# Attention and two feed-forwards on one core: a leaky ramp for the weights' first pass, one-step low parts, a gate from the hyperbolic tangent, and a new order

## The chip, the cores and the metric

The kernel runs on one core of a Trainium2 chip. The metric is the time of one execution on the device in microseconds (us), lower being better. Engines are named as the profile names them: PE (TensorE), DVE (VectorE), ACT (ScalarE), POOL (GpSimd) and SP (SyncE, which here issues nearly all transfers).

## The reference

Attention with RMS-normed q and k, then a feed-forward with a SiLU gate (width 2048), then a second one with a SiLU gate times a value branch (width 1536):

```python
def _attn_ref(q, k, v, g_q, g_k):                 # (4 batches, 12 heads, 448 rows, 64)
    q_n, k_n = (rmsnorm(q, g_q), rmsnorm(k, g_k))
    scores = scale * np.matmul(q_n, k_n.transpose(0, 1, 3, 2))
    attn = np.exp(scores - np.max(scores, axis=-1, keepdims=True))
    return np.matmul(attn / (np.sum(attn, axis=-1, keepdims=True) + 1e-09), v)

def _moe_ref(x, w_in, w_out):                     # x is 1792 x 768, d_ff 2048
    h = x @ w_in
    return h * (1.0 / (1.0 + np.exp(-h))) @ w_out

def _moe2_ref(x, w_gate, w_val, w_out):           # d_ff 1536
    g = x @ w_gate
    return g * (1.0 / (1.0 + np.exp(-g))) * (x @ w_val) @ w_out
```

The five weight matrices arrive as 64-bit floats, the rest as 32-bit ones.

## The kernel before

Every large product is made from float16 parts: each operand is a high part plus a low part, and three products of parts stand for one. So the other engines have two jobs beside softmax and gates: to make parts of every operand, and to turn the 64-bit weights into 32-bit ones.

**Stages.** Attention of batch 0 runs first (its products are in float32), then the hidden half of the first feed-forward for batch 0 (`ffn1_h(0)`, 288 matmuls), which needs all of `w_in` in parts, then its output half (`ffn1_o(0)`), which needs all of `w_out`. From there on, the attention of batch b+1 runs between the matmuls of `ffn1_o(b)` and `ffn1_h(b+1)`. After the last batch comes the second feed-forward, in blocks of 512, 512, 384 and 384 tokens: block 0 by `ffn2_gv`, the others by `ffn2_seven`, which makes four products out of seven with the help of precomputed sums of weights (`make_sums`, which writes `s2d`, and `make_parts`, which writes `t2d`; both are made while blocks 0 and 1 run). `ffn2_out` closes each block.

**The weights' first pass** (`bring`, lines 998 to 1034) takes a staged block of 64-bit words as pairs of 32-bit ones. A multiply of the upper word by 2^-112 (lines 1013 to 1015, on ACT, DVE or POOL) leaves the fraction in place for a shift by three bits. The sign is lost in that shift and is carried beside it: in form "D" by two DVE instructions (a mask, line 1019, and a shift of a half word, line 1020), otherwise by one DVE shift (line 1023) and two instructions of 768 on ACT or POOL (lines 1029 and 1030). Line 1032 puts shift and rest together, line 1034 sums squares for the scale. `bring` handles 1536 words a partition at a time for `w_in` and `w_out` (8 each) and 768 for the 36 blocks of the second feed-forward.

**Low parts of weights** (`convert`, `split`): on DVE (line 979), on POOL, or, in form "E", as PE pieces of 384 columns (lines 795 and 796, a float32 product and one by the constant tile `NI`), each emptied by ACT (line 798).

**Gate of the first feed-forward** (`ffn1_h`): ACT reads a finished PSUM bank with Silu (line 1161), scales into a high part (1166), and DVE makes the low part (1174). Exponentials of softmax (line 860) and Silu live in different ACT tables, so a change between the two costs an `ACT_TABLE_LOAD`. Three PSUM banks serve `ffn1_h` and `ffn1_o` in turn.

**Low parts in the second feed-forward** take three instructions: high part on ACT (1417, 1586), difference on DVE (1418, 1587), scaling by 2^11 on ACT or POOL (1420, 1589).

**Order.** `Plan.emit` lists every engine's instructions in advance, from assumed durations, from due times and from the tables of numbers in `TUNE`; tables such as `WOL` also say which engine may take an operation (A, D, P for ACT, DVE, POOL; E for PE). Each engine then runs its list in that order. Where the list would leave PE idle for longer, the planner puts in filler products (line 1811: `NI` by itself, 512 columns, no result used).

Of the kernel before, what the change touches and what calls it, by code (L numbers as in the profile page):

```python
# [1846 lines left out]
```

## Time and profile before

| | us |
|---|---|
| median of three runs | 1187.19 |
| lowest, highest | 1184.96, 1190.58 |
| the profiled execution's own time | 1184.59 |
| its span, first to last instruction | 1182.8 |
| PE busy in the span | 1140.7 (96%) |
| DVE, ACT, POOL busy | 917.6, 749.7, 260.6 |

A busy PE is not all useful work here: fillers, and PE pieces that make low parts, count as busy. The mean granted clock is 0.996 of full speed. The stages can be told by PE's lines: float32 attention to 112 us, `ffn1_h(0)` from 112 to 185, PE pieces for `w_out` from 169 to 211, `ffn1_o(0)` from 211, the first matmul of `ffn2_gv` at 657, of `ffn2_seven` at 847.

### The profile page before, as it was taken

The page shows a single profiled execution, that of the slowest core. Times are in us where ns is not written, and L with a number is a line of the kernel's source. Part 1 is how long each engine was busy: PE and PEld are TensorE (multiplying, and loading weights), DVE is VectorE, ACT ScalarE, POOL GpSimd, SP SyncE. Part 2 cuts the span into 40 slices and gives each one's busy share as a digit, 9 for nine tenths or more (in the row PEclk, how much of TensorE's full clock was granted, in tenths as well). Part 3 has the DMA queues.
Part 4 walks back from the last instruction along what each step waited for, and adds up shares of the span by engine and source line. Part 5 has one row for each costly group of instructions (what it writes and reads, how often), then busy time and mean ns, then how long its engine had stood idle before and what let it go on. Part 6 is the DMA issues. An engine that isn't in the chain of part 4 may idle for free.

```text
span 1182.8 us, 20080 instructions
## 1 busy us (share of the span) xinstructions
PE 1140.7 (96%) x7400; PEld 675.8 (57%) x7400; DVE 917.6 (78%) x1762; ACT 749.7 (63%) x1288; POOL 260.6 (22%) x231
## 2 busy tenths in 40 slices
PE   8999998999999999999999999999999899999998
PEld 4444544454444445454555554445688668987995
DVE  5989988988588876885379978877999866774773
ACT  4888978887599856995468667574356531441440
POOL 4585222245344524531031021000000000000000
PEclk9999999999999999999999999999999899999999
DMA  9555755689979997776756878646787675463432
GB/s 212 160 132 146 242 202 154 111 193 189 201 158 180 184 203 163 149 139 136 260 176 200 295 250 298 217 157 199 237 255 249 231 247 168 161 190 117 168 130 67
DMA packets 271315, 222.59 MB, mean 188 GB/s; under 512 B 187120, under 2 KB 246000, under 8 KB 271216
## 3 DMA queue, kind: packets, MB, share of 16 engines
q1 hardware_dynamic: 271056, 221.10, 68.0%
q8 instruction: 58, 0.95, 0.3%
q14 instruction: 41, 0.34, 0.1%
q10 hardware_dynamic: 160, 0.20, 0.0%
HBM read 140.44 MB, written 38.14 MB: 151 GB/s over the span
## 4 chain that ended last, share of the span: by engine, by line
PE 34%; DMA 9%; DVE 7%; ACT 5%; issue 2%; SPq 1%; POOL 1%; ACTq 0%; DVEq 0%; POOLq 0%
PE ps L1529 12%; PE ps L1643 9%; PE ps L1155 5%; PE ps L1195 4%; DMA ATT<-y2d 3%; PE ps L1407 2%; DMA ATT<-in_moe_w_out_dram 2%; DMA t2d<-ATT 1%; DMA ATT<-s2d 1%; DMA ATT<-in_moe_w_val_dram 1%; DVE ATT L979 1%; PE ps L951 1%; ACT ATT L1034 1%; DMA ATT<-x2d 1%; PE ps L841 1%
## 5 line engine op out<-in xcount | busy, mean ns | idle before, releaser
L1155 PE MATMUL ps<-XT,W 128*128 128x448 f16 x1152 | 232.5, 352 | 2.5 <-ACT FD L1161 2.3
L1195 PE MATMUL ps<-G,W 128*128 128x448 f16 x1152 | 233.4, 352 | 1.5 <-ACT FD L1199 1.1
L1155 PEld LDWEIGHTS <-W 128*128 128x128 f16 x1152 | 112.0, 98 | 108.1 <-issue 7.9
L1195 PEld LDWEIGHTS <-W 128*128 128x128 f16 x1152 | 111.9, 98 | 108.1 <-issue 6.0
L1529 PEld LDWEIGHTS <-ATT 128*128 128x128 f16 x1458 | 130.8, 99 | 16.4 <-issue 6.5
L1529 PE MATMUL ps<-XT,ATT 128*128 128x192 f16 (+1 forms) x972 | 122.0, 257 | 6.8 <-ACT G L1549 5.7
L860 ACT ACTIVATE ER<-ps,ST 128x448 f32<-128x448 f32 x144 | 102.0, 712 | 12.2 <-DVE ATT L884 5.0
L1643 PEld LDWEIGHTS <-G 128*128 128x128 f16 x720 | 70.3, 98 | 46.9 <-issue 0.3
L1643 PE MATMUL ps<-W,G 128*128 128x384 f16 x528 | 95.8, 326 | 0.1
L851 DVE TENSOR_REDUCE ST<-ps 128x2 f32<-128x896 f32 (+1 forms) x96 | 91.7, 965 | 5.3 <-PE ps L820 2.5
L884 DVE SCALAR_TENSOR_TENSOR ATT<-ER,ST,ATT 128x448 f16<-128x448 f32 x114 | 81.1, 729 | 3.5 <-ACT ATT L876 2.8
L1407 PE MATMUL ps<-XT,W 128*128 128x512 f16 x360 | 81.6, 379 | 1.3 <-ACT FD L1199 0.6
L1529 PEld LDWEIGHTS <-W 128*128 128x128 f16 x810 | 73.0, 98 | 8.3 <-issue 3.1
L1529 PE MATMUL ps<-XT,W 128*128 128x192 f16 (+1 forms) x540 | 73.2, 256 | 2.7 <-DVE ATT L1656 1.8
L1529 PE MATMUL ps<-ER,ATT 128*128 128x192 f16 (+1 forms) x486 | 66.5, 257 | 0.0
L1407 PEld LDWEIGHTS <-W 128*128 128x128 f16 x360 | 35.2, 98 | 43.1 <-issue 3.0
L841 PE MATMUL ps<-ATT 128*128 128x448 f16 x216 | 55.3, 353 | 3.7 <-ACT ER L860 2.9
L694 POOL TENSOR_TENSOR ST<-ST 128x14 f32<-128x14 f32 x20 | 55.9, 2797 | 1.4
L1174 DVE SCALAR_TENSOR_TENSOR G<-FD,ST,G 128x448 f16<-128x448 f32 x64 | 46.7, 743 | 7.0 <-POOL G L1168 4.6
L1546 DVE TENSOR_TENSOR FD<-ps,FD 128x192 f32<-128x192 f32 (+3 forms) x90 | 41.3, 464 | 11.2 <-PE ps L1529 9.2
L1656 DVE SCALAR_TENSOR_TENSOR ATT<-ps,ST,ATT 128x384 f32<-128x384 f32 x46 | 27.6, 614 | 23.9 <-ACT ATT L1652 23.3
L951 PE MATMUL ps<-ATT 128*64 128x448 f16 x396 | 42.2, 355 | 4.0 <-DMA ATT<-ATT 4.0
(283 smaller groups left out, 2123.8 us busy)
## 6 DMA issues: line engine op xcount, KB each, us to landing
ATT<-s2d SPq DMA_DIRECT2D x36, 768.0 KB, 4.3
ATT<-in_moe_w_out_dram SPq DMA_DIRECT2D x24, 768.0 KB, 6.6
ATT<-t2d SPq DMA_DIRECT2D x36, 384.0 KB, 3.6
W<-in_moe_w_in_dram SPq DMA_DIRECT2D x16, 768.0 KB, 6.5
ATT<-in_moe_w_gate_dram SPq DMA_DIRECT2D x12, 768.0 KB, 5.7
ATT<-in_moe_w_val_dram SPq DMA_DIRECT2D x12, 768.0 KB, 5.5
y2d<-ATT SPq DMA_DIRECT2D x24, 384.0 KB, 2.9
ATT<-y2d SPq DMA_DIRECT2D x12, 768.0 KB, 5.8
```

Of the source, the lines that this page charges most:

```text
L694: op(POOL, 2600, lambda: nc.gpsimd.tensor_tensor(st["r"], st["r"], half, ALU.pow), shared=False, r=["half"], w=[("r", i)], due=due)
L841: nc.tensor.matmul(out=sp[:, u, 0:S], lhsT=T[:, 0, t, :], rhs=T[:, a, :, 64 * h:64 * h + 64], start=(a == 1), stop=(a == 2))
L851: op(DVE, 1.04 * S * nt + 65, lambda sp=sp, top=top, nt=nt: nc.vector.tensor_reduce(top, sp[:, 0:nt, 0:S], AX.X, ALU.max, negate=True), r= ...
L860: op(ACT, 705, lambda e=e, u=u, t=t, sp=sp, own=own: nc.scalar.activation(e, sp[:, u, 0:S], AF.Exp, bias=st["nb"][:, t:t + 1], scale=1.0 i ...
L884: DVE: (t_stt(S), lambda e=e, hi=hi, lo=lo, r1=r1: nc.vector.scalar_tensor_tensor(lo, e, r1, hi, ALU.mult, ALU.subtract), True),
L951: nc.tensor.matmul(out=PS_X[64 * h:64 * h + 64, 0:S], lhsT=vv[:, h, b, :], rhs=PT[:, b].rearrange("p t c -> p (t c)")[:, S * h:S * h + S], ...
L1155: nc.tensor.matmul(out=ps[:, 0:S], lhsT=w[:, a, kk], rhs=xt1((b * HP + kk) % NX, x), start=(kk == 0 and s == 0), stop=(kk == KD - 1 and s ...
L1174: DVE: (t_stt(S), lambda gt=gt, hi=hi, lo=lo, s1=s1: nc.vector.scalar_tensor_tensor(lo, gt, s1, hi, ALU.mult, ALU.subtract), True),
L1195: nc.tensor.matmul(out=ps[:, 0:S], lhsT=w[:, a, P * m:P * m + P], rhs=GV1[:, f, x], start=(f == 0 and s == 0), stop=(f == NF1 - 1 and s == 2))
L1407: nc.tensor.matmul(out=ps[:, 0:n], lhsT=w[:, aa, kk], rhs=xt2(kk, x)[:, 0:n], start=(kk == 0 and s == 0), stop=(kk == KD - 1 and s == 2))
L1529: nc.tensor.matmul(out=ps[:, h * o:h * o + h], lhsT=w[:, aa, kk], rhs=XW[kk][:, c:c + h], start=(kk == 0 and s == 0), stop=(kk == KH - 1 a ...
L1643: nc.tensor.matmul(out=ps[:, bank, 0:384], lhsT=lh[a], rhs=rh[b], start=(x == 0 and (bank, a, b) != (1, 1, 0)), stop=(x == m - 1 and (bank ...
```

## The change

1. **The weights' first pass.** The multiply becomes a leaky ramp (`Prelu`) on ACT alone. A negative number gets a further factor of 2^32, which puts a one where the shift by three makes it the sign. The instructions that carried the sign go, and with them the choice of engine:

```diff
@@ def bring
-        add(only(wy, {
-            ACT: (t_act(n) + 150, lambda: nc.scalar.activation(y, hw.bitcast(F32), AF.Copy, scale=2.0 ** -112)),
-            DVE: (0.525 * n + 77, lambda: nc.vector.tensor_scalar(y, hw.bitcast(F32), 2.0 ** -112, None, ALU.mult), True),
-            POOL: (1.15 * n, lambda: nc.gpsimd.tensor_scalar(y, hw.bitcast(F32), 2.0 ** -112, 1.0, ALU.mult, ALU.mult))}),
...
-        if sign == "D":
-            half_words = stage.bitcast(U16).rearrange("p (n t) -> p n t", t=4)
-            op(DVE, 0.525 * n + 67, lambda: nc.vector.tensor_scalar(hw, hw, -0x80000000, None, ALU.bitwise_and), ...
-            op(DVE, 1.04 * n + 145, lambda: nc.vector.tensor_scalar(half_words[:, :, 2], half_words[:, :, 1], 13, ...
...
+        op(ACT, t_act(n) + 150, lambda: nc.scalar.activation(y, hw.bitcast(F32), AF.Prelu, scale=2.0 ** -112, alpha=2.0 ** 32), ...
+        op(DVE, 0.525 * n + 67, lambda: nc.vector.tensor_scalar(lw, lw, 29, None, ALU.logical_shift_right), ...
+        op(DVE, 1.04 * n + 71, lambda: nc.vector.scalar_tensor_tensor(yi, yi, 3, lw, ALU.logical_shift_left, ALU.bitwise_or), ...
```

2. **The gate in batches 1 to 3.** Silu becomes a hyperbolic tangent of half the argument, and DVE finishes it from the bank: (tanh + 1) times the sum. The halves go into the scales `dh` and `sg`. Batch 0 keeps Silu.

```diff
@@ def ffn1_h
-            op(ACT, 518, lambda ps=ps, gt=gt, f=f: nc.scalar.activation(gt, ps[:, 0:S], AF.Silu, scale=dh[:, f:f + 1]), ... table="silu")
+            op(ACT, 518, lambda ps=ps, gt=gt, f=f: nc.scalar.activation(gt, ps[:, 0:S], AF.Tanh if b else AF.Silu, ... table="exp" if b else "silu")
+            if b:
+                op(DVE, t_stt(S), lambda ps=ps, gt=gt: nc.vector.scalar_tensor_tensor(gt, gt, 1.0, ps[:, 0:S], ALU.add, ALU.mult), ...
```

3. **One-step low parts in the second feed-forward.** The high part is scaled by 2^-11 as ACT writes it, and one DVE instruction gives the low part. The third instruction goes (72 of them).

```diff
@@ def ffn2_seven (ffn2_gv alike)
-                op(ACT, t_act(m), lambda src=src, hi=hi: nc.scalar.activation(hi, src, AF.Copy), r=sk, w=[hk], due=-1e4)
-                op(DVE, t_tt(m), lambda src=src, hi=hi, rest=rest: nc.vector.tensor_tensor(rest, src, hi, ALU.subtract), ...
-                add({POOL: (t_pts(m), lambda rest=rest, lo=lo: nc.gpsimd.tensor_scalar(lo, rest, 2.0 ** 11, 1.0, ...
-                     ACT: (t_act(m), lambda rest=rest, lo=lo: nc.scalar.activation(lo, rest, AF.Copy, scale=2.0 ** 11))},
+                op(ACT, t_act(m), lambda src=src, hi=hi: nc.scalar.activation(hi, src, AF.Copy, scale=2.0 ** -11), ...
+                op(DVE, t_stt(m), lambda src=src, hi=hi, lo=lo: nc.vector.scalar_tensor_tensor(lo, hi, -2.0 ** 11, src, ALU.mult, ALU.add), ...
```

4. **A new order.** The tables of `TUNE` are replaced, some of the planner's assumed durations change, and it no longer reckons with fetches of instructions by DMA. Two lines of the tables:

```diff
@@ TUNE
-    WOL=('E', 'E', 'E', 'E', 'E', 'E', 'E', 'E'),
+    WOL=('E', 'DP', 'E', 'D', 'E', 'DP', 'E', 'D'),
-    PHI2=('AD', 'P', 'AD', 'A', 'AD', 'AP', 'D'),
+    PHI2=('A', 'ADP', 'A', 'A', 'A', 'A', 'A'),
```

In counts of instructions over the whole program: PE pieces for low parts of weights 36 before and 20 after, fillers 86 and 96, all other matmuls alike; ACT table loads 44 and 4; DVE instructions 97 fewer; high parts of softmax on ACT 58 and 101, on DVE 46 and 12; their low parts on POOL 12 and 37, on DVE 114 and 89; multiplies by the gain of k on POOL 4 and 32.

On ACT, where `ffn1_h(1)` runs between softmax tiles of batch 2, before (L1161 is the gate, L860 the exponentials, L715 a high part of q and k):

```order
L1161 ACT_TABLE_LOAD
L1161 ACTIVATE FD<-ps,ST 128x448 x2
L860 ACT_TABLE_LOAD
L860 ACTIVATE ER,ST<-ps,ST 128x448 x4
L715 ACTIVATE ATT<-SQ 128x14x64
```

After (L1127 is the gate, L842 the exponentials, L858 and L1134 high parts of softmax and gate, L672 squares):

```order
L672 ACTIVATE SQ<-ATT 128x896
L858 ACTIVATE ATT<-ER,ST 128x448 x3
L842 ACTIVATE ER,ST<-ps,ST 128x448
L1127 ACTIVATE FD<-ps,ST 128x448 x2
L842 ACTIVATE ER,ST<-ps,ST 128x448
L1134 ACTIVATE G<-FD,ST 128x448 x2
```

The loads around each gate are gone, and gates and exponentials alternate tile by tile.

On PE, shortly ahead of the first matmul of `ffn1_o(0)`, before (L795 and L796 are a PE piece, L533 the maximum over the scales of `w_out`, L1811 a filler):

```order
L795 MATMUL ps<-XT,FD 128x384
L796 LDWEIGHTS NI
L796 MATMUL ps<-W,NI 128x384
L533 MATMUL ps<-ID,ST 128x128
L1811 LDWEIGHTS NI
L1811 MATMUL ps<-NI 128x512
```

After (L777 and L778 are a PE piece, L823 scores of batch 1; the maximum over the scales, now L515, follows behind these rows):

```order
L777 MATMUL ps<-XT,FD 128x384
L778 LDWEIGHTS NI
L778 MATMUL ps<-W,NI 128x384
L823 LDWEIGHTS ATT
L823 MATMUL ps<-ATT 128x448
```

Before, four PE pieces and one filler stand between the maximum and the first output matmul; after, the pieces are done ahead of the maximum, and ten fillers (L1773) and a few scores stand behind it. From the last matmul of `ffn1_h(0)` to the first of `ffn1_o(0)` PE has 21 pieces and 17 fillers before, 8 and 30 after; inside `ffn1_h(0)` it has 11 pieces before and 8 after.

On PE in `ffn2_seven` of block 1, after (L1494 is a product, L1773 a filler):

```order
L1494 MATMUL ps<-XT,ATT 128x256
L1494 LDWEIGHTS ATT
L1494 MATMUL ps<-ER,ATT 128x256
L1773 LDWEIGHTS NI
L1773 MATMUL ps<-NI 128x512
```

Seventeen fillers in four groups stand among the 756 products of that block; before it had none.

## Rows read from the trace of the kernel before

**Rows 1.** The page's first part: busy time, share of the span, instructions.
```profile
PE 1140.7 (96%) x7400; PEld 675.8 (57%) x7400; DVE 917.6 (78%) x1762; ACT 749.7 (63%) x1288; POOL 260.6 (22%) x231
```

**Rows 2.** Busy time by stretch: length, PE, PEld, DVE, ACT, POOL, clock, DMA share, GB/s.
```profile
0.00:112.00 112.00, 101.53 (x573) 49.20 (x574) 90.16 (x144) 86.69 (x181) 67.71 (x59) 1.00 0.66 171
112.00:168.70 56.70, 55.73 (x297) 28.50 (x295) 53.93 (x79) 47.04 (x61) 16.37 (x9) 1.00 0.56 185
168.70:211.00 42.30, 38.31 (x144) 17.85 (x143) 34.18 (x55) 34.58 (x55) 8.72 (x8) 1.00 0.51 170
211.00:300.00 89.00, 86.05 (x504) 42.87 (x502) 76.53 (x160) 69.56 (x153) 37.53 (x35) 1.00 0.90 175
300.00:328.00 28.00, 25.33 (x141) 12.66 (x140) 14.66 (x24) 14.98 (x24) 9.79 (x13) 1.00 0.99 196
328.00:850.00 522.00, 515.11 (x2832) 261.16 (x2830) 408.19 (x781) 368.65 (x588) 120.52 (x111) 1.00 0.74 199
850.00:947.00 97.00, 89.06 (x768) 76.12 (x767) 88.98 (x189) 54.05 (x88) 0.00 (x0) 0.96 0.77 245
```

**Rows 3.** PE in order of time, two PE pieces: start, length, instruction.
```profile
168.76 0.81 PE L795 MATMUL ps<-W,FD 128*128 128x384 f32 x2
169.41 0.33 PE L796 MATMUL ps<-W,NI 128*128 128x384 f16 x1
169.57 0.81 PE L795 MATMUL ps<-W,FD 128*128 128x384 f32 x2
```

**Rows 4.** Groups by line, 0 to 211 us: count, busy us, mean ns, idle before.
```profile
L1020 DVE TENSOR_SCALAR ATT<-ATT 128x1536 uint16<-128x1536 uint16 x6 | 11.4, 1898 | 0.1
L1019 DVE TENSOR_SCALAR ATT<-ATT 128x1536 int32<-128x1536 int32 x6 | 5.8, 968 | 0.1
L1014 DVE TENSOR_SCALAR W<-W 128x1536 f32<-128x1536 f32 x4 | 4.3, 1068 | 0.7 <-DMA W<-in_moe_w_out_dram 0.7
L979 DVE SCALAR_TENSOR_TENSOR W<-W,ST 128x1536 f16<-128x1536 f32 x6 | 10.8, 1804 | 0.0
L1030 POOL TENSOR_SCALAR W<-W 128x768 f16<-128x768 f32 x10 | 20.9, 2087 | 16.5 <-DVE W L1023 15.9
L1013 ACT ACTIVATE W<-W 128x1536 f32<-128x1536 f32 x3 | 5.0, 1650 | 0.8 <-DMA W<-in_moe_w_out_dram 0.4 <-ACT ATT L776 0.4
L1034 ACT ACTIVATE W<-W 128x1536 f32<-128x1536 f32 x10 | 14.8, 1484 | 6.9 <-DVE W L1032 5.7 <-issue 1.2
```

**Rows 5.** Groups by line on ACT, whole span.
```profile
L1161 ACT ACT_TABLE_LOAD x22 | 28.2, 1283 | 0.8 <-DMA x2d<-FD 0.4
L860 ACT ACT_TABLE_LOAD x21 | 26.9, 1283 | 0.6 <-DVE ATT L884 0.3
```

**Rows 6.** PE in order of time, 300 to 328 us.
```profile
306.22 4.26 PE L1811 MATMUL ps<-NI 128*128 128x512 f16 x19
312.12 2.24 PE L951 MATMUL ps<-ATT 128*64 128x448 f16 x21 [1.33 <-DMA ATT<-ATT]
```

**Rows 7.** DVE groups by line, whole span; then PE's waits: total, times, longest.
```profile
L961 DVE SCALAR_TENSOR_TENSOR XT<-ps,XT 128x448 f16<-128x448 f32 x18 | 11.1, 619 | 14.7 <-ACT XT L956 14.7
L851 DVE TENSOR_REDUCE ST<-ps 128x2 f32<-128x896 f32 x72 | 77.4, 1082 | 3.6 <-PE ps L820 2.5 <-PE ps L841 0.9
...
PE ps L1155 <- ACT FD L1161: 2.3, 3, 1.3
```

**Rows 8.** Block 1: DVE's busiest stretch, ACT, PE, the clock behind the gap.
```profile
875.00:900.00 25.00, 24.19 (x221) 21.30 (x219) 24.86 (x56) 15.18 (x27) 0.00 (x0) 1.00 0.81 257
...
860.71 0.78 ACT L1486 ACTIVATE ATT<-W,ST 128x576 f16<-128x576 f32 x1 [6.07 <-DMA t2d<-ATT]
...
925.53 1.86 PE L1529 MATMUL ps<-XT,ATT 128*128 128x256 f16 x8 [4.86 <-ACT G L1549]
...
926.00:928.00 2.00, 2.00 (x11) 1.39 (x10) 2.00 (x7) 2.00 (x3) 0.00 (x0) 0.50 0.86 350
```

**Rows 9.** Groups by line on ACT, whole span: one form of the third low-part instruction.
```profile
L1589 ACT ACTIVATE W<-W 128x384 f16<-128x384 f32 x22 | 11.3, 520 | 6.8 <-DVE W L1587 6.8
```

More of the change, by code (lines that the diff above doesn't have):

```diff
@@ L145, in __init__ @@
         self.filler = None
-        self.products = {}
     def bank(self, key, ap):
@@ L158, in short, with add @@
         self.drains[j] = i
-    def add(self, alts, r=(), w=(), due=0.0, late=0.0, table=None, cont=False, count=3):
+    def add(self, alts, r=(), w=(), due=0.0, late=0.0, table=None, cont=False):
         i = len(self.ops)
-        self.products[i] = count
         for key in set(r) | set(w):
@@ L338, in emit @@
                 self.taken[i].append(key)
-            if e == PE:
-                streamed += self.products[i]
-                while streamed >= fetch:
-                    fetches.append(t0)
-                    fetch += step
             fn()
@@ L919, in row_scales @@
         ps, pk = psf()
-        op(PE, 800, lambda: nc.tensor.matmul(out=ps[:, 0:S], lhsT=BO, rhs=DR_0, start=True, stop=True), r=["vl", "vh"], w=[pk], due=due - 500, count=2)
+        op(PE, 800, lambda: nc.tensor.matmul(out=ps[:, 0:S], lhsT=BO, rhs=DR_0, start=True, stop=True), r=["vl", "vh"], w=[pk], due=due - 500)
         rt, rtk = ft()
@@ L936, in pv @@
                             start=(b == 0), stop=(b == 3))
-            op(PE, 3300, pv, r=[(V_0K[n > 0], u) for u in range(3)] + [("pt0", n % 2, t) for t in range(J)], w=["psx"], due=due - 1000, count=16)
+            op(PE, 3300, pv, r=[(V_0K[n > 0], u) for u in range(3)] + [("pt0", n % 2, t) for t in range(J)], w=["psx"], due=due - 1000)
             xf, xk = row_scales(n, due)
@@ L953, in pv @@
                         start=(s == 0), stop=(s == len(steps) - 1))
-        op(PE, 2480, pv, r=["vh", "vl"] + [("PT", t) for t in range(J)], w=["psx"], due=due - 1000, count=22)
+        op(PE, 2480, pv, r=["vh", "vl"] + [("PT", t) for t in range(J)], w=["psx"], due=due - 1000)
         scale = 2.0 ** -14
@@ L996, with bring @@
     LEAST, MOST = 2.0 ** -15 * (1 + 0x100000 / 2.0 ** 23), 2.0 ** 16 * (1 + 0x6FFFFF / 2.0 ** 23)
-    def bring(srcs, stage, skeys, y, ykeys, sumcol, sumkey, due, need, claim=(), wy="AP", sign="A"):
+    def bring(srcs, stage, skeys, y, ykeys, sumcol, sumkey, due, need, claim=()):
         m = len(srcs)
@@ L1074, in load_w_in @@
             plan.part = ("w_in", p)
-            bring([cols_of(w_in, P * (f + u), P) for u in range(2)], stage, skeys, y, ykeys, ss_in[:, f:f + 1], ("ssi", p), need - 20, need, wy=TUNE["WIY"][p], sign=TUNE["WIS"][p])
+            bring([cols_of(w_in, P * (f + u), P) for u in range(2)], stage, skeys, y, ykeys, ss_in[:, f:f + 1], ("ssi", p), need - 20, need)
             g = slice(f, f + 2)
@@ L1103, in load_w_out @@
                 y, yk = XT[:, 2 * S * x:2 * S * x + 3072].bitcast(F32), [(k, u) for u in range(x, x + 4) for k in ("xh", "xl")]
-            bring([rows_of(w_out, P * (c + u)) for u in range(2)], st, stk, y, yk, ss_o1[:, c:c + 1], ("sso", p), need - 10, need, claim=["att0"], wy=TUNE["WOY"][p], sign=TUNE["WOS"][p])
+            bring([rows_of(w_out, P * (c + u)) for u in range(2)], st, stk, y, yk, ss_o1[:, c:c + 1], ("sso", p), need - 10, need, claim=["att0"])
             g = slice(c, c + 2)
@@ L1160, in ffn1_h @@
             last = f == NF1 - 1
-            op(ACT, 518, lambda ps=ps, gt=gt, f=f: nc.scalar.activation(gt, ps[:, 0:S], AF.Silu, scale=dh[:, f:f + 1]),
-               r=[pk, ("dh", f)], w=[gk] + ([("silu", b)] if last else []), due=-1e4, table="silu")
+            op(ACT, 518, lambda ps=ps, gt=gt, f=f: nc.scalar.activation(gt, ps[:, 0:S], AF.Tanh if b else AF.Silu, scale=dh[:, f:f + 1]),
+               r=[pk, ("dh", f)], w=[gk] + ([("silu", b)] if last else []), due=-1e4, table="exp" if b else "silu")
+            if b:
+                op(DVE, t_stt(S), lambda ps=ps, gt=gt: nc.vector.scalar_tensor_tensor(gt, gt, 1.0, ps[:, 0:S], ALU.add, ALU.mult), r=[pk], w=[gk] + ([("silu", b)] if last else []), due=-1e4)
             hi, lo = GV1[:, f, 0], GV1[:, f, 1]
@@ L1667, in store @@
             for rows, src in parts:
-                move(400, 1300, 1500, lambda rows=rows, src=src: nc.sync.dma_start(out=rows, in_=src),
+                move(400, 800, 1540, lambda rows=rows, src=src: nc.sync.dma_start(out=rows, in_=src),
                      r=[("ot", o, 0), ("ot", o, 1)], due=-1e4)
```

150 lines of the change are left out of this document (60 added, 90 removed), and 76 rows, old and new, of the table NUDGE.

## The prediction

> **What bounds the kernel now.** I read the page's first part first: PE is busy for 1140.7 of 1182.8 us, DVE for 917.6, ACT for 749.7, POOL for 260.6 [rows 1]. So the time is PE's list plus PE's idle time, 42.1 us, and the other engines count only where PE waits for them or works in their place. Second, the windows by stage [rows 2], PE's busy time against the length: 10.5 us idle before the first feed-forward (0 to 112), 1.0 inside `ffn1_h(0)`, 4.0 from 168.7 to 211, 3.0 up to 300, 2.7 from 300 to 328, 6.9 from 328 to 850, 7.9 in the first 97 us of block 1, the rest behind. Third, what PE does while it is "busy". In the third of these stretches the pace is that of PE pieces: one starts at 168.76 and the next at 169.57 [rows 3], 0.81 us each, for work that is no product of the reference. Fillers are the other busy time without use: 19 of them take 4.26 us ahead of a PV product that then still waits 1.33 for a DMA [rows 6].
>
> So for this change the questions are: how many PE pieces and fillers does the new list hold, and which of PE's waits does it move? Time taken from ACT, DVE or POOL is worth nothing by itself.
>
> **The change part by part.** All sums are against the profiled execution's own 1184.6 us (1182.8 span plus 1.8 around it); the median of the three runs is 2.6 us higher, and that is added at the end.
>
> **PE pieces.** There are 36 before and 20 after, all else on PE but fillers being alike. Sixteen pieces at the pace of 0.81 us [rows 3] are 13.0 us. This lies on the path: from 168.7 to 211 PE is busy for 38.3 of 42.3 us [rows 2], nearly all of it pieces and fillers, and the first matmul of `ffn1_o(0)` stands behind them. The pieces become 4 low parts of 1536 words for DVE or POOL, 1.80 us each on DVE [rows 4], 7.2 us if all went there; with others that the tables move to DVE it is about 14. These need room, which the first pass gives back: in the first 211 us DVE loses the sign's two instructions (6 of 1.898 and 6 of 0.968 us, 17 us) and multiplies (4 of 1.068, 4 us, and two in another form); a shift of about the length of the mask comes back for each former form "D". POOL loses its half-word instructions, 10 of 2.087 us, 20.9 [rows 4]. With the smaller steps of attention that the tables move off DVE I count the order's instructions at these durations: DVE 191 us before, 168 after; ACT 198 and 186; POOL 28 less. So the helpers have room for the conversions, and the path gets shorter by the pieces' time. The cover is DVE's 211 minus 168 us: if it failed, the o-stage would wait for a conversion and one would cost 1.8 us.
>
> **Fillers up to `ffn1_o(0)`.** 62 before and 66 after; fourteen more of them stand in the last gap, where the pieces stood, and ten fewer before `ffn1_h(0)`. One takes about 0.22 us (19 in 4.26 [rows 6]). A filler in a wait is free, one in front of a ready product costs its time; I charge all four: +0.9. Together with the pieces -12.1: `ffn1_o(0)` starts at about 199 instead of 211.
>
> **The stall at 306.** Before, 24 fillers and a wait of 1.33 us [rows 6] stand there, since the DMA queues are full (share 0.99 from 300 to 328 [rows 2]). After, 13 fillers: 11 fewer, 2.4 us. If the transfers still end as late as before relative to PE, the fillers turn into waiting and nothing is won; if the sooner `ffn1_o(0)` runs into the same transfers, it is worse by as much as the stage came forward. The DMA rate is set by the list of loads, which also moves forward as buffers come free sooner. I take -2.4, bounds 0 and -2.4.
>
> **Block 1 of the second feed-forward.** Its list gets 17 fillers, 3.7 us, where before had none. PE waits there today: 4.86 us for a gate at 925.5, and behind that gap the granted clock is at 0.50 (1.2 GHz) in the stretch 926 to 928 [rows 8]; over the 97 us the mean is 0.96 [rows 2], so about 3.2 to 3.9 us are lost to the lower level on top of the gap. DVE runs at 24.86 of 25 us [rows 8] from 875 to 900, its list for the whole stretch hardly changes (95.0 us before, 96.9 after, in the same counting: 48 low parts from two instructions to one but two more shifts and parts), while ACT falls from 51 to 40. ACT's 6.07 us at 860.7 is a wait for DMA [rows 8]. So the bound there, DVE and the transfers, stays; fillers in a wait keep PE active. Ends: all 17 on top, +3.7; all waits and the clock's loss gone, -11. I take -1.6, half of the smaller loss at the lower clock, since DVE's sum [rows 8] speaks for the gap to stay.
>
> **Third low-part instruction.** 72 of them go; 22 on ACT of 520 ns with 6.8 us of idle time before them, all on DVE [rows 9]. They stand where ACT has slack: nothing, or a piece of the -1.6.
>
> **Tables and tanh.** The 22 and 21 loads, 28.2 and 26.9 us of ACT [rows 5], nearly all go. ACT is busy for 369 of 522 us from 328 to 850, PE idle for 6.9 [rows 2]: they are covered by that slack, and what is late is seen in PE's waits on banks held by the gate: 2.3 us in three waits [rows 7]. The new DVE instruction, 48 times, isn't in the trace. Its nearest row is L961, which reads a bank in the same shape, 619 ns [rows 7]; 30 us more DVE in a stretch where it has 408 of 522 [rows 2], less 97 instructions elsewhere. Bounds: -2 (those waits gone) to +30 (none covered, a rival below). I take -1.
>
> **Prelu for Copy.** Not in the trace; the nearest row is the same pass as a Copy, 1650 ns for 1536 [rows 4]. I take it equal; at double, 16 passes before 211 us would cost 26 us more, all of the 25 (211 minus 186) that ACT has free there. It moves 6 or so multiplies of the first 211 us from DVE or POOL to ACT.
>
> **The sum.** -13.0 + 0.9 - 2.4 - 1.6 - 1.0 = -17.1, so 1167.5 for the profiled execution and 1170 for the median.
>
> **The rivals.**
>
> *Larger gain (1156).* Freed helpers also take away PE's idle time. For it: much of that is waiting for exactly these engines. 0 to 211: 15.5 us idle, and with a third left to start-up and half of the rest gone it is -5; block 1's waits gone, net of what I took, about -5.3; half the idle time from 328 to 850 and a little [rows 2] -4. Sum -14.3. Against it: DVE is nearly full in block 1, and the DMA share is near 1 from 211 to 328.
>
> *Little gain (1181).* ACT becomes the bound before `ffn1_h(0)`. In the order 8 pairs of `w_in` are handled ahead of the first gate where it was 6, and all multiplies are ACT's: its sum there is 124 us against 116, in a stage with ACT busy for 86.7 of 112 [rows 2]. If ACT sets that stage, it grows in proportion, 8 x 86.7/116 = +6; with block 1's fillers on top, +3.7 in place of -1.6, it is 1170 + 6.0 + 5.3 = 1181, and 1184 if the stall at 306 stays as well (+2.4). Against it: ACT is idle for 25 us there, and its squares wait 5.7 us for DVE [rows 4], which is relieved.
> The Trainium skill, "ScalarE: Activation LUTs", section "Rules for kernel authors", says that simple multiplies belong on VectorE rather than ScalarE. The trace agrees on the price: 1650 ns on ACT against 1068 on DVE [rows 4]. By that rule, the ten passes moved from DVE make each load chain some 0.6 us longer, and this rival is where it would show.
>
> *Slower (1199).* A gate's bank used to be free after Silu; now it is held until DVE's turn comes. DVE may then be in a reduce of 1.08 us [rows 7] or have several ahead. Behind it would be PE's next group of 18 matmuls, and what is queued on DVE behind that instruction, the maxima of scores above all. At 0.62 us for each of 48 groups, uncovered, it is +30: 1170 + 30 = 1199 or so. It decides from 17/48 = 0.35 us a group on. For it: PE already waits on a bank held by the gate [rows 7]. Against it: three banks in turn, and a group of 18 matmuls at 55.73/297 = 0.19 us [rows 2] gives 3.4 us for a bank to come free, 6.8 with the spare one.
>
> That the change doesn't do what it says I leave out: the order shows 4 loads and 20 pieces.
>
> **How the numbers follow.** Forecast 0.50, larger gain 0.25, little gain 0.17, slower 0.08. The likeliest is the forecast, 1170. The range reaches from 1153, a little under the larger gain, to 1183, over the little gain's lower end, and leaves out the slower case, half the little gain's upper end and the tail below. A measurement of this kernel tells about 0.5% from no change, 1181.3 to 1193.1. Faster by more: the forecast, the larger gain and some 0.07 of the little gain, 0.82; within 0.5%: 0.10; slower: 0.08.
>
> **What would show each step.** Right: `ffn1_o(0)` starting near 199; 20 pieces, 4 loads; `Prelu` near 1.65 us; the tanh's DVE instruction under 0.7 us with no PE wait for it; 13 fillers and at most 1.3 us of waiting at the old stall; in block 1 a PE idle near 8 us with less time at the lower clock. Wrong: `ffn1_h(0)` starting after 114 with ACT full ahead of it; PE waiting for a conversion before `ffn1_o(0)`; waits of PE on banks that DVE still holds; fillers directly in front of ready products, without a wait behind them. A gain that lies outside the first 211 us would make my reason wrong even at the right time.

## The result, and the profile after

The changed kernel takes 1165.85 us (median of four runs, 1164.25 to 1168.07). Its ratio to the kernel before is 0.9847, 95% interval 0.9804 to 0.9889: 18 us sooner, with some 5 us of uncertainty either way (the plain medians, 1186.08 of four runs of the kernel before and 1165.85, lie 20 us apart). The forecast was 1170, range 1153 to 1183. The profiled execution's span is 1163.9 us against 1182.8, 18.9 us less.

The first part of the page after, to be held against [rows 1]:

```profile
PE 1126.1 (97%) x7362; PEld 673.2 (58%) x7362; DVE 882.5 (76%) x1665; ACT 680.3 (58%) x1241; POOL 283.0 (24%) x266
```

PE is busy for 14.6 us less and idle for 37.8 us instead of 42.1, which is 4.3 us less. Together these are the 18.9 us. The new instructions cost what their nearest rows said. Groups by line of the kernel after (count, busy us, mean ns, idle before): the gate's second instruction, and the leaky ramp on a block of 1536.

```profile
L1130 DVE SCALAR_TENSOR_TENSOR FD<-FD,ps 128x448 f32<-128x448 f32 x48 | 29.2, 615 | 12.9 <-ACT FD L1127 12.6
L994 ACT ACTIVATE W<-W 128x1536 f32<-128x1536 f32 x10 | 16.5, 1648 | 0.2 <-DVE W L961 0.2
```

615 ns against the 619 of L961, and 1648 against the 1650 of the Copy [rows 4, 7].

Stretches of the kernel after, cut at its own stages (up to the first matmul of `ffn1_h(0)`, to its last, to the first of `ffn1_o(0)`, and block 1 of the second feed-forward); columns as in [rows 2]:

```profile
0.00:109.60 109.60, 99.38 (x571) 49.30 (x572) 88.68 (x144) 92.31 (x187) 49.80 (x53) 1.00 0.70 186
109.60:175.90 66.30, 66.30 (x339) 34.12 (x339) 61.55 (x82) 58.42 (x78) 26.11 (x19) 1.00 0.68 227
175.90:191.40 15.50, 15.03 (x63) 6.94 (x62) 14.04 (x26) 11.95 (x19) 2.16 (x2) 1.00 0.43 89
823.60:978.80 155.20, 144.19 (x1147) 112.18 (x1145) 125.03 (x257) 52.73 (x80) 0.00 (x0) 0.97 0.70 230
```

The same cuts in the kernel before, from its matmul records. Block 1 is cut in both at the first product of `ffn2_seven` and at the same product of block 2, some 13 us behind block 2's first:

| | before, us | after, us | difference |
|---|---|---|---|
| up to the first of `ffn1_h(0)` | 112.2 | 109.6 | -2.6 |
| `ffn1_h(0)` | 72.5 | 66.3 | -6.2 |
| from there to the first of `ffn1_o(0)` | 26.2 | 15.5 | -10.7 |
| **first matmul of `ffn1_o(0)` at** | **210.9** | **191.4** | **-19.5** |
| from there to block 1 | 635.7 | 632.2 | -3.5 |
| block 1 | 148.9 | 155.2 | +6.4 |
| the rest | 187.3 | 185.1 | -2.3 |

The whole gain is made in the first 191 us. Behind that, 3.5 us are won ahead of block 1 and 2.3 after it, and 6.4 are lost in block 1. (The first row moves by 2 us from one execution to another of the same instructions: 108.0 to 109.8 in the eight kernels of this document that have the order of after and are alike up to there.) Inside `ffn1_h(0)` PE is idle for 2.1 us before and never after.

### The profile page after: what moved, and what is told of

It reads as the page before. It is cut to its first block, busy times and chain, and to the rows that moved or that the text cites. A ratio compares the mean times of both kernels' runs of the same rounds, so it can differ in the third digit from the quotient of the medians.

```text
span 1163.9 us, 19864 instructions
## 1 busy us (share of the span) xinstructions
PE 1126.1 (97%) x7362; PEld 673.2 (58%) x7362; DVE 882.5 (76%) x1665; ACT 680.3 (58%) x1241; POOL 283.0 (24%) x266
## 4 chain that ended last, share of the span: by engine, by line
PE 66%; DMA 9%; DVE 8%; ACT 5%; issue 3%; SPq 3%; POOL 1%; DVEq 0%; ACTq 0%; POOLq 0%
PE ps L1121 14%; PE ps L1163 13%; PE ps L1494 12%; PE ps L1605 10%; PE ps L1375 8%; DMA ATT<-ATT 3%; PE ps L823 2%; PE ps L933 2%; DMA t2d<-ATT 2%; DMA ATT<-in_v_dram 2%; DMA ATT<-y2d 1%; PE ps L916 1%; DVE ATT L866 1%; ACT ER L842 1%; SPq L870 1%
## 5 line engine op out<-in xcount | busy, mean ns | idle before, releaser
L1494 PEld LDWEIGHTS <-ATT 128*128 128x128 f16 x1458 | 131.3, 99 | 22.5 <-issue 11.2
L1494 PE MATMUL ps<-XT,ATT 128*128 128x192 f16 (+1 forms) x972 | 120.3, 259 | 10.1 <-ACT G L1514 6.1
L842 ACT ACTIVATE ER<-ps,ST 128x448 f32<-128x448 f32 x144 | 102.4, 714 | 10.3 <-POOL ATT L864 5.1
L1375 PE MATMUL ps<-XT,W 128*128 128x512 f16 x360 | 85.0, 379 | 0.0
L1494 PEld LDWEIGHTS <-W 128*128 128x128 f16 x810 | 72.9, 98 | 6.0 <-issue 0.6
L866 DVE SCALAR_TENSOR_TENSOR ATT<-ER,ST,ATT 128x448 f16<-128x448 f32 x89 | 65.6, 755 | 7.6 <-ACT ATT L858 6.2
L1494 PE MATMUL ps<-XT,W 128*128 128x192 f16 (+1 forms) x540 | 70.2, 255 | 0.4 <-DVE FD L1511 0.4
L858 ACT ACTIVATE ATT<-ER,ST 128x448 f16<-128x448 f32 x101 | 63.5, 662 | 9.0 <-DVE ST L850 3.2
L1494 PE MATMUL ps<-ER,ATT 128*128 128x192 f16 (+1 forms) x486 | 66.6, 258 | 0.6 <-DVE ER L961 0.6
L823 PE MATMUL ps<-ATT 128*128 128x448 f16 x216 | 56.1, 353 | 6.0 <-ACT ER L842 4.2
L1127 ACT ACTIVATE FD<-ps,ST 128x448 f32<-128x448 f32 x64 | 39.9, 629 | 17.7 <-PE ps L1121 13.8
```

The source lines that it names most:

```text
L823: nc.tensor.matmul(out=sp[:, u, 0:S], lhsT=T[:, 0, t, :], rhs=T[:, a, :, 64 * h:64 * h + 64], start=(a == 1), stop=(a == 2))
L842: op(ACT, 705, lambda e=e, u=u, t=t, sp=sp, own=own: nc.scalar.activation(e, sp[:, u, 0:S], AF.Exp, bias=st["nb"][:, t:t + 1], scale=1.0 i ...
L858: ACT: (t_act(S, False, 1), lambda e=e, hi=hi, r1=r1: nc.scalar.activation(hi, e, AF.Copy, scale=r1)),
L866: DVE: (t_stt(S), lambda e=e, hi=hi, lo=lo, r1=r1: nc.vector.scalar_tensor_tensor(lo, e, r1, hi, ALU.mult, ALU.subtract), True),
L1375: nc.tensor.matmul(out=ps[:, 0:n], lhsT=w[:, aa, kk], rhs=xt2(kk, x)[:, 0:n], start=(kk == 0 and s == 0), stop=(kk == KD - 1 and s == 2))
L1494: nc.tensor.matmul(out=ps[:, h * o:h * o + h], lhsT=w[:, aa, kk], rhs=XW[kk][:, c:c + h], start=(kk == 0 and s == 0), stop=(kk == KH - 1 a ...
```

## The experiments

Two theories stand against each other for the first 191 us. **Piece theory**, my prediction's: PE pieces are on the path, each piece that goes gives its 0.81 us back. **Chain theory**: the first output matmul waits for the first pass of the last pairs of `w_out` (load, ramp, merge, sum of squares; a pair is 1536 words a partition), then for the maximum over the scales and the scaling of the gate; pieces stand in that wait. Most kernels below keep the order of before, or of after, word for word: an edit replaces what an entry of the list gives out, and the planner reckons as if nothing had changed. Ratios are to the kernel before, run beside each kernel (medians of 1182 to 1183 us there). Several intervals overlap with that of the changed kernel; where they do, a reading rests on the stages of the traced executions.

### Parts of the change in the order of before

**The ramp alone** (the sign's instructions give out nothing):

```diff
-        ACT / DVE / POOL: y = upper word * 2^-112
+        ACT, at that place of the order: nc.scalar.activation(y, hw, AF.Prelu, scale=2.0 ** -112, alpha=2.0 ** 32)
```

> The kernel before with the leaky ramp as the weights' first pass and nothing else; every other instruction stays where it was in each engine's list, the 36 PE pieces and 86 fillers too. Theory 1 (only what PE's list holds counts, relief of DVE, ACT and POOL by itself is worth nothing): 0 to -2 us. Theory 2 (PE's idle time in the first 211 us, 15.4 us, is waiting for helpers, and their relief takes half of what is not start-up): -4 to -6 us, first matmul of the first output half at about 206 in place of 210.9.

Measured 1192.15 us, ratio 1.0083 (1.0054 to 1.0111): 9 us *longer*. Neither theory had a loss. PE waits for ACT to empty its pieces for 8.6 us, 4.1 before: the multiplies of DVE and POOL now stand in ACT's list as well. For the last two pairs DVE waits 5.54 and 4.72 us for ACT's sums of squares, 1.80 and 1.64 before.

**Low parts on DVE for 16 pieces, without the ramp:**

```diff
-        4 PE pieces of 384 columns, each emptied by ACT   (every second pair of w_out)
+        nc.vector.scalar_tensor_tensor(lo, y2, s1, hi, ALU.mult, ALU.subtract)   # in place of the first piece
```

> The kernel before with the low parts of every second pair of w_out made by one DVE instruction of 1536 words (4 in all) in place of 16 PE pieces, at the same place of the list; the sign of the weights is still carried by DVE. Theory 1 (pieces are pure PE time on the path): -13 us. Theory 2 (DVE has no room: it is busy 53.9 of 56.7 us from 112 to 168.7 and 34.2 of 42.3 behind, and 4 x 1.8 = 7.2 us more come later than the pieces did): -4 to -8 us.

Measured 1188.33 us, ratio 1.0046 (1.0031 to 1.0061): no gain, a small loss. PE in order of time, in brackets what it waited for:

```profile
183.58 1.65 PE L795 MATMUL ps<-W,FD 128*128 128x384 f32 x2 [6.11 <-ACT W L798]
...
203.63 1.07 PE L795 MATMUL ps<-XT,FD 128*128 128x384 f32 x2 [4.29 <-POOL FD L1047]
...
213.90 0.73 PE L1196 MATMUL ps<-G,W 128*128 128x448 f16 x3 [3.16 <-DVE G L1186]
```

The last low part on DVE, between the maximum and that scaling:

```profile
211.10 1.82 DVE L1065 SCALAR_TENSOR_TENSOR W<-XT,ST,W 128x1536 f16<-128x1536 f32 x1 [0.25 <-ACT W L967]
```

Where pieces stood PE now waits: 11.5 us of idle time between the two halves instead of 2.9, and `ffn1_o(0)` (the last row) starts at 213.9 instead of 210.9, for the scaled gate on DVE. So the pieces' time isn't given back one for one. That no piece was on the path this run doesn't show: the edit also puts low parts on DVE ahead of the scaling, and with PE idle the mean granted clock of the gap falls to 0.87 (1.00 before).

**Both, and all edits of the code**, in the order of before (for the second, the gate and the low parts of the second feed-forward as in the diff ahead of the prediction; only the new order is missing):

> The two edits together: ramp, and 4 low parts on DVE in place of 16 PE pieces, in the order of before. Theory 1: -13 to -15 us, and the same as the low parts alone. Theory 2: the ramp makes the room, so more than the sum of the two alone, -13 to -18 us, and the first matmul of the first output half at 195 to 198.

> All four edits of the code (ramp, 4 low parts on DVE for 16 PE pieces, gate from the hyperbolic tangent in batches 1 to 3, one-step low parts) in the order of before, with its 86 fillers. If the new order adds nothing of its own, this is -17 to -20 us, as the changed kernel. If table loads and third low-part instructions lie beside other work (my forecast), it is 0 to -2 us from the run with ramp and low parts. If the gate's bank, held until DVE's turn, stops PE, it is slower than that run by up to 30 us.

Both: 1185.65 us, ratio 1.0019 (1.0004 to 1.0035); again the last low part (1.81 us) stands between the maximum and the scaling, PE waits 2.81 us for that, and the gap's mean granted clock is 0.84. All: 1194.56 us, ratio 1.0095 (1.0069 to 1.0120). The gate from the hyperbolic tangent costs 9.7 us between the first and the last output matmul of the first feed-forward (516.4 us against 506.8 with ramp and low parts only), 7.9 of them up to the last `ffn1_h`; behind the last output matmul, where the one-step low parts are, some 1.3 come back. PE's waits with all edits (total, times, longest), where L1178 are the matmuls of `ffn1_h` and L1187 the gate's second instruction:

```profile
PE ps L1178 <- DVE FD L1187: 6.7, 15, 1.0
...
PE ps L1222 <- DVE FD L1187: 1.6, 2, 0.9
```

This is the mechanism of my slower rival, on a smaller scale. The kernel after has no such wait among its own. So all edits of the code, in the old order, make it 11 us slower; with the new order it is 18 us faster.

### The chain ahead of the first output half

The chain itself, DVE in order of time, before (L1014 the multiply of the last pair but one into XT, L1032 the merges, L534 the maximum, L1185 the scaling of the gate) and then after (L996, L516, L1153):

```profile
191.20 0.96 DVE L1014 TENSOR_SCALAR XT<-ATT 128x1536 f32<-128x1536 f32 x1
195.12 1.76 DVE L1032 SCALAR_TENSOR_TENSOR XT<-XT,ATT 128x1536 int32<-128x1536 int32 x1
202.23 1.76 DVE L1032 SCALAR_TENSOR_TENSOR XT<-XT,ATT 128x1536 int32<-128x1536 int32 x1
207.36 0.29 DVE L534 TENSOR_REDUCE ST<-ps 128x1 f32<-128x128 f32 x1 [0.88 <-PE ps L533]
208.25 5.52 DVE L1185 TENSOR_SCALAR G<-G,ST 128x896 f16<-128x896 f16 x15
```

```profile
177.33 1.76 DVE L996 SCALAR_TENSOR_TENSOR XT<-XT,ATT 128x1536 int32<-128x1536 int32 x1
180.72 1.76 DVE L996 SCALAR_TENSOR_TENSOR XT<-XT,ATT 128x1536 int32<-128x1536 int32 x1
185.79 1.82 DVE L961 SCALAR_TENSOR_TENSOR W<-XT,ST,W 128x1536 f16<-128x1536 f32 x1
188.56 0.29 DVE L516 TENSOR_REDUCE ST<-ps 128x1 f32<-128x128 f32 x1 [0.87 <-PE ps L515]
190.44 1.89 DVE L1153 TENSOR_SCALAR G<-G,ST 128x896 f16<-128x896 f16 x5
```

The ramp of that pair after, on ACT:

```profile
174.79 1.67 ACT L994 ACTIVATE XT<-ATT 128x1536 f32<-128x1536 f32 x1
```

And what stands directly ahead of the first output matmul, before (between the two rows lie 3.5 us of pieces) and then after:

```profile
207.37 0.81 PE L795 MATMUL ps<-XT,FD 128*128 128x384 f32 x2
...
210.87 0.73 PE L1195 MATMUL ps<-G,W 128*128 128x448 f16 x3
```

```profile
189.36 1.98 ACT L1154 ACTIVATE G<-G,ST 128x896 f16<-128x896 f16 x2 [0.91 <-DVE ST L1082]
```

```profile
191.38 2.81 PE L1163 MATMUL ps<-G,W 128*128 128x448 f16 x14
```

After, ACT starts the ramp of that pair at 174.8, 1.1 us ahead of the end of `ffn1_h(0)`; before, the multiply came 6.6 us behind it. From there to the first output matmul it is 16.6 us instead of 19.7. 7.7 and 3.1 are, to the rounding, the 10.7 us of the table.

The chain wasn't the whole of the gap before. The first of the fifteen scalings, the one that the first output matmul reads, takes 0.45 us and is done at 208.7; PE comes to that matmul at 210.87, straight from its pieces. So for the last 2.2 us pieces stood in front of ready work. After, that matmul reads a gate scaled by ACT (the second of the two, done at 191.3) and starts at 191.38, as the last filler ends. Of the 10.7 us, 8.5 are the chain and 2.2 pieces.

**The old sign pass on the last two pairs, in the changed kernel:**

```diff
+        nc.vector.tensor_scalar(hw, hw, -0x80000000, None, ALU.bitwise_and)           # pairs 6 and 7 of w_out
+        nc.vector.tensor_scalar(half_words[:, :, 2], half_words[:, :, 1], 13, None, ALU.logical_shift_right)
         nc.vector.scalar_tensor_tensor(yi, yi, 3, hw, ALU.logical_shift_left, ALU.bitwise_or)
```

> The changed kernel with the old sign pass on the last two pairs of w_out alone: Copy in place of the ramp, and two DVE instructions more (0.96 and 1.89 us) ahead of the merge, the shift left out; order, pieces and fillers as in the changed kernel. Chain theory: DVE's part of the last two pairs gets 2.85 us longer each, and the first output half starts 4 to 5.5 us later (196 in place of 191.4), all of it kept to the end. Piece theory: PE has 30 fillers in that gap, the chain has room, 0 to 1 us.

DVE of that kernel: the merges (L1006) end later, and so does the scaling of the gate (L1166); ahead of it DVE waits for the maximum (L516), a product of PE. Then two rows of PE's last four pieces:

```profile
179.23 1.76 DVE L1006 SCALAR_TENSOR_TENSOR XT<-XT,ATT 128x1536 int32<-128x1536 int32 x1
...
184.49 1.76 DVE L1006 SCALAR_TENSOR_TENSOR XT<-XT,ATT 128x1536 int32<-128x1536 int32 x1
...
193.92 0.29 DVE L516 TENSOR_REDUCE ST<-ps 128x1 f32<-128x128 f32 x1 [2.47 <-PE ps L515]
...
195.80 4.43 DVE L1166 TENSOR_SCALAR G<-G,ST 128x896 f16<-128x896 f16 x12
```

```profile
188.10 0.91 PE L777 MATMUL ps<-XT,FD 128*128 128x384 f32 x2 [2.48 <-POOL FD L1024]
...
189.01 1.44 PE L777 MATMUL ps<-XT,FD 128*128 128x384 f32 x2
```

The scaling comes at 195.80 instead of 190.44 and `ffn1_o(0)` at 196.7 instead of 191.4: +5.4, with the same pieces and fillers. The span is 1168.9 us, +5.0; the median of the runs is 1169.46, +3.6 (ratio 0.9874, 0.9839 to 0.9908). The chain theory's number was 4 to 5.5, but it was met in part by luck. It reckoned 2.85 us a pair and didn't take off the shift of 0.95 us that the edit leaves out: DVE's part grows by 1.9 us a pair, 3.8 in all. By that much PE starts its last four pieces later (188.10 instead of 184.32). They are of the last pair but one and stand ahead of the maximum in PE's list, and now they take 5.0 us instead of 3.4: PE was idle for 2.48 us ahead of them, and from 188 to 193 the mean granted clock is 0.66, part of it at 1.2 GHz. So 3.8 us are the chain on DVE, and 1.6 are pieces that the chain goes through.

**The chain sooner in the order of before** (ramp and low parts on DVE as above, and the first pass of the last four pairs of `w_out` earlier in the lists):

```diff
+ SP, ACT, DVE: load, ramp, shift, merge, squares and scale of pairs 4, 5, 6, 7 stand 6, 8, 12, 14 us earlier, by the planner's times
```

> The run with ramp and 4 low parts on DVE in the order of before, and on top of it only the first pass of the last four pairs of w_out (loads, ramp, shift, merge, sum of squares, scale) 6 to 14 us earlier in the lists of SP, ACT and DVE. Chain theory (the first output matmul waits for the last pairs' first pass, the maximum over the scales behind it and the scaling of the gate; PE pieces only stood in that wait): the first output half starts at 200 to 205 in place of 211.2, and the whole run is 6 to 10 us shorter than that run, about 1176 to 1180. Piece theory (what counts is PE's own list): no change from 1185.7, within 2 us.

Measured 1196.80 us, ratio 1.0111 (1.0081 to 1.0141): `ffn1_o(0)` starts at 221.5, 10 us *later*, a miss for both theories. The loads had not landed: ACT stood 6.06 and 5.35 us in front of the two ramps into XT, with the gates of `ffn1_h(0)` and the emptying of pieces behind it in its list. PE waited for an emptying behind the first of them, and 4.83 us behind the second:

```profile
192.56 1.65 PE L832 MATMUL ps<-W,FD 128*128 128x384 f32 x2 [13.41 <-ACT W L835]
```

So the chain begins at the load, whose staging buffer comes free when the pair two ahead has had its squares taken (the two staging buffers serve in turn): those end at 181.5, and the ramp starts at 187.56, when the load has landed. An earlier place in a list alone doesn't shorten it.

**The chain put first in the order of after**, and 27 fillers left out (10 behind the maximum, 17 in block 1):

```diff
 PE:   piece, piece, [maximum over the scales], piece, piece, scores, [no fillers], first output matmul
 DVE:  scales, [no parts of the last pair here], maximum, scaling of the gate, parts of the last pair
```

> The changed kernel with the chain ahead of the first output half put first in DVE's and PE's lists: the maximum over the scales goes ahead of two PE pieces, the high and the low part of the last pair of w_out (1.02 and 1.82 us of DVE) and a softmax maximum (1.08) go behind the scaling of the gate, and the 10 fillers behind the maximum and the 17 of block 1 are left out. Chain theory: the first output half starts 2.0 to 2.8 us sooner (about 189 in place of 191.4) and with the fillers of block 1 gone (-1.9 in the run before) the whole is 3.5 to 4.5 us shorter than the changed kernel, about 1161.5. If PE's pieces set that start, it stays within 0.5 us of 191.4 and only the -1.9 shows.

Measured 1161.52 us, ratio 0.9825 (0.9807 to 0.9843), the shortest here that does all the work; it is 4 us under the changed kernel, but the two intervals overlap. The gap from `ffn1_h(0)` is 14.0 us instead of 15.5, a gain of 1.5 where 2.0 to 2.8 were expected: DVE waits 1.49 us for the maximum, 0.87 in the changed kernel, since two pieces are still ahead of it on PE. The stage behind the gap is 3.1 us longer, mostly idle time of PE (6.2 us against 3.6), and the first matmul of `ffn1_h(1)` comes at 266.6 instead of 266.7: nothing is left of the gain. Of the span's 5.0 us, 3.1 are block 1's, and 2.4 lie between, where no edit stands.

**Fillers of the gap left out** (30):

```diff
     def filler(ps, count):
+        given[0] += count
+        if 36 < given[0] <= 66:
+            return
```

> The changed kernel without the 30 fillers between the hidden and the output half of batch 0. Chain theory: the fillers stand in a wait, the first output half still starts at 191 to 192 with PE idle some 6 us more; if the granted clock falls to 1.2 GHz in the gap, the matmuls behind it are slower and up to 3 us are lost. If fillers were on the path, it starts 2 to 6 us sooner.

Measured 1164.24 us, ratio 0.9849 (0.9828 to 0.9869). `ffn1_o(0)` starts 18.2 us behind `ffn1_h(0)`, 2.7 later than with fillers. The window that holds the gap, with a mean granted clock of 0.80, part of it at 1.2 GHz; with fillers it is 1.00:

```profile
175.00:192.00 17.00, 12.44 (x39) 6.03 (x37) 12.29 (x20) 10.99 (x16) 3.71 (x2) 0.80 0.43 101
```

How it comes about, on PE and on DVE:

```profile
184.38 1.65 PE L777 MATMUL ps<-XT,FD 128*128 128x384 f32 x2 [1.43 <-POOL FD L1011]
```

```profile
191.48 0.29 DVE L516 TENSOR_REDUCE ST<-ps 128x1 f32<-128x128 f32 x1 [3.73 <-PE ps L515]
```

PE is idle for 2.28 us ahead of its last piece but four and for 1.43 ahead of the last four, these take 6.3 us instead of 3.4, and the maximum behind them in PE's list comes 2.7 us later. So these fillers stood in waits and paid for themselves: they kept the clock up for pieces that the chain goes through. The total doesn't show it: 2.3 of the 2.7 us are left at the start of block 1, and block 1 was shorter in this execution, by as much as it varies (below).

### The gate and the order

**Silu again, in the order of after:**

```diff
-            nc.scalar.activation(gt, ps, AF.Tanh, scale=dh)  and  nc.vector.scalar_tensor_tensor(gt, gt, 1.0, ps, ALU.add, ALU.mult)
+            nc.scalar.activation(gt, ps, AF.Silu, scale=dh)      # dh without its half, sg as before
```

> The changed kernel with Silu back as the gate of batches 1 to 3 and the 48 instructions of DVE behind it gone, in the order of the changed kernel: 54 table loads in place of 4, so 50 x 1.283 = 64 us more on ACT between 267 and 650 us, and some 30 us less on DVE. If table loads lie beside other work in any order (my forecast's term of -1 us): within 3 us of the changed kernel, 1165 to 1169. If the new order, where gates and exponentials alternate tile by tile, needs a gate without a load: 10 to 40 us longer than it, with PE waiting for exponentials and for banks held by the gate.

Measured 1218.74 us, ratio 1.0308 (1.0286 to 1.0330), some 53 us more than the changed kernel. ACT's groups and PE's largest wait (L842 the exponentials):

```profile
L1127 ACT ACT_TABLE_LOAD x27 | 34.6, 1283 | 1.1 <-PE ps L1121 0.5
L842 ACT ACT_TABLE_LOAD x26 | 33.4, 1283 | 0.5
```

```profile
PE ps L823 <- ACT ER L842: 44.8, 26, 3.5
```

So in the order of after, the tangent is worth 53 us, and in the order of before it costs 10. An order that alternates gates and exponentials tile by tile pays only with a gate that needs no load. The Trainium skill, "ScalarE: Activation LUTs", section "Rules for kernel authors", says to group functions by their table set and finish one set before switching; these runs agree, with 4 loads and 54.

### Block 1 of the second feed-forward

**Its 17 fillers left out:**

```diff
     def filler(ps, count):
+        given[0] += count
+        if given[0] > 79:
+            return
```

> The changed kernel without the 17 fillers of block 1 of the second feed-forward; all else alike. If they stand in front of ready products (my little-gain rival), 2.5 to 3.7 us shorter. If they stand in waits and keep the clock up, 0 to 2 us longer, since the stretches at 1.2 GHz behind the 3.0 and 5.6 us gaps grow. If they stand in waits and the clock falls anyway, 0.

Measured 1163.66 us, ratio 0.9835 (0.9804 to 0.9866). The block takes 153.4 us instead of 155.2, and PE's idle time grows from 11.0 to 14.7 us, by about the fillers' own time. The 1.9 us aren't clear of the spread: the same instructions, with all 17 fillers, take 154.5, 153.4 and 152.9 us in three kernels whose edits lie elsewhere (the old sign pass, no fillers in the gap, Silu). So the fillers stood in waits for the most part, and that they cost anything isn't shown.

**The last three sums later:**

```diff
+ DVE, ACT: all of weight_sums(f) behind its load, for f = 10, 5, 11 (the last three), stands 4, 5.5, 5.5 us later, by the planner's times
```

> The changed kernel with the last three sums of weights (f = 10, 5, 11) 4.0, 5.5 and 5.5 us later in the lists of DVE and ACT, so that DVE no longer stops for their loads (3.48 and 1.31 us) while finished banks wait behind. If DVE's order is what stops PE in block 1: the gap of 3.0 us there goes and the block is 3 to 6 us shorter (155.2 before this edit). If DVE's sum of work is the bound there, only the place of the gap moves, within 1 us.

Measured 1176.80 us, ratio 0.9955 (0.9930 to 0.9980): the block grows to 169.3 us, a miss for both numbers. PE's wait for the loads of the finished sums (`s2d`) goes up to 10.5 us, in four waits; it was 0.6. The sums had no slack: each one starts with a load into the one buffer that the sum ahead still works in.

**Without the last five loads for the sums:**

```diff
-        move(420, 2600, 2650, lambda: nc.sync.dma_start(out=Y..., in_=y2d[...]))
+        move(420, 2600, 2650, lambda: f in (4, 5, 9, 10, 11) or nc.sync.dma_start(out=Y..., in_=y2d[...]))
```

> The changed kernel without the last five loads for the sums of weights (f = 9, 4, 10, 5, 11; those sums are made from what lies in the buffer, so five sums are wrong), all instructions of the engines and the 17 fillers kept. If the pace of these loads (6 to 11 us to land, DVE waits 7.0 us for them in block 1) is what made block 1 longer than before, the two large gaps of PE (3.0 and 5.6 us) shrink by half or more and the block falls from 155.2 to 147 to 150. If DVE's sum of work sets it, 153 to 155.

Measured 1160.09 us, ratio 0.9812 (0.9794 to 0.9831). The block takes 148.6 us, with all its fillers: as long as before the change (148.9; 146.1 to 148.9 in the six kernels with the old order), and shorter than in all four kernels of the new order that leave the block unedited (152.9 to 155.2). The first instruction of a sum, groups by line in block 1: before, after, and without the loads. The last figure is DVE's idle time ahead of it.

```profile
L1288 DVE TENSOR_TENSOR ATT<-ATT 128x384 f32<-128x384 f32 x4 | 2.2, 556 | 0.2 <-DMA ATT<-y2d 0.2
```

```profile
L1256 DVE TENSOR_TENSOR ATT<-ATT 128x384 f32<-128x384 f32 x5 | 2.8, 557 | 7.0 <-DMA ATT<-y2d 7.0
```

```profile
L1256 DVE TENSOR_TENSOR ATT<-ATT 128x384 f32<-128x384 f32 x5 | 2.7, 549 | 0.0
```

And where it hurts after, DVE and then PE in order of time:

```profile
877.26 0.56 DVE L1256 TENSOR_TENSOR ATT<-ATT 128x384 f32<-128x384 f32 x1 [3.48 <-DMA ATT<-y2d]
```

```profile
880.65 2.08 PE L1494 MATMUL ps<-XT,ATT 128*128 128x256 f16 x9 [3.04 <-DVE FD L1511]
...
908.88 2.08 PE L1494 MATMUL ps<-XT,ATT 128*128 128x256 f16 x9 [5.59 <-ACT G L1514]
```

Block 1 comes 23 us sooner than before, the sums only 0.4 to 16 us (the first at 730.6 instead of 747.0, the tenth at 877.3 instead of 877.7): five of twelve are left when it starts, instead of four, and DVE stands 7.0 us in front of their loads with finished banks behind it in its list. Leaving the loads out also takes five transfers of 768 KB off the queue (DMA share 0.65 instead of 0.70), so what DVE's waits and what the busier queue cost isn't told apart. The 5.6 us gap stays at 4.8 without the loads, and the kernel before has it too, 4.86 [rows 8]; its cause, in the pair of gates ahead of it, is open.

## Why the prediction was right in time, and which of its steps failed

**PE pieces and fillers up to `ffn1_o(0)`: right sign, too small, and for the most part the wrong mechanism.** Predicted -12.1 and a start at 199, measured -19.5 and 191.4. The step that failed is "the first matmul of `ffn1_o(0)` stands behind them": that PE is busy for 38.3 of 42.3 us [rows 2] was read as a path. Of the sixteen pieces' 13.0 us the traces show some 4.6 on it: 2.2 at the end of the gap, and about 2.4 for three pieces inside `ffn1_h(0)`, where PE has no idle time after. The rest was a wait filled with work. What shortens the gap is the chain: the last pair but one begins its first pass 7.7 us sooner, measured from the end of `ffn1_h(0)`, and has 1.9 us less of DVE in series, which the prediction had only as room on DVE. That the chain sets the start is shown by the longer sign pass, 3.8 us. What the 7.7 us owe to the edits and what to the new order is open; an earlier place in the old order's lists didn't give them.

The prediction's cover said that, if DVE's room failed, one conversion would cost 1.8 us. In both orders one does stand in the chain: 1.82 us ahead of the scaling with the low parts moved in the old order, and 1.82 us (at 185.79, in the rows above) ahead of the maximum in the new one. The run that put the chain first moved it back, and gained 1.5 us in all up to `ffn1_o(0)`.

**Counts.** Some of the prediction's counts for the first 211 us are short, without an effect on its sum. The trace has nine blocks in form "D" there, not six (26 us of DVE's two instructions, not 17), and eleven multiplies that move to ACT, seven from DVE and four from POOL, where it says 6 or so in one place and ten from DVE in another. The gap before holds 16 fillers in the trace, so the "fourteen more" of the prediction is right, and the 17 ahead of it isn't.

**Prelu at the Copy's price, the gate's instruction at 0.62 us: right**, 1648 and 615 ns. That giving ACT all the multiplies can cost time shows in the old order, where the ramp alone is 9 us longer; in the new one the stage ahead of `ffn1_h(0)` is no longer than before.

**Tables and tanh, -1.** From the first output matmul to block 1 the kernel is 3.5 us shorter, near the -3.4 of this term and the next together, but no run tells them apart from the order. The step was too simple in both directions: some 53 us hang on the tangent in the new order, and in the old order it costs 10.

**The slower rival** has its mechanism in the old order, half as strong as it would need: 8.3 us in 17 waits are 0.17 us for each of 48 groups, and it decides from 0.35. In the new order there is none of it.

**Larger and little gain.** PE's idle time fell by 4.3 us, where the larger gain asked for 14.3. `ffn1_h(0)` started at 109.6, not after 114, with ACT busy for 92.3 of 109.6 us ahead of it.

**The stall at 306.** 13 fillers stand there after, and the wait behind them is 0.73 us, both as forecast; between the first matmuls of `ffn1_h(1)` and `ffn1_o(1)` PE is idle for 3.1 us, 4.1 before. That the -2.4 was won there isn't shown: this stretch is 2.0 us longer than before (87.1 against 85.1), with other products in it.

**Block 1: the term that was mis-sized.** Predicted -1.6, bounds -11 and +3.7; measured +6.4, and +4.0 at the least by the executions above, outside both. The sums' loads are 4.3 to 6.6 us of the block in the new order; a part of the fillers isn't shown. [Rows 8] show DVE full from 875 to 900, but that the sums' loads were nearly late no row could tell: DVE waited 0.2 us for them. The prediction asked of the stall at 306 whether the transfers come sooner too, and not of block 1.

**The total was right by luck.** Up to `ffn1_o(0)` the gain was 7.4 us more than predicted, in block 1 8.0 less, elsewhere 2.4 more (-5.8 against -3.4). So the profiled execution came to 1165.84 against 1167.5; the 2.6 us added for the median were not there, and the median came within 4 us of 1170.

## What to carry to other kernels

A busy stretch of an engine is not yet a path: look at when the inputs of the first instruction behind it were ready, and follow that back over the other engines, before counting busy time as gain. Here that gives 2.2 us for the pieces of the gap, and the rest for the chain. Edits and order are one change: here the edits are 11 us slower in the old order and 18 us faster in the new one, so the value of a part can't be read from a kernel that is not ordered for it. When a stage comes forward, ask of every transfer that it uses whether it comes forward as well.
